# GpSimd makes the shifted copies of VectorE's exponentials with 64-bit integer adds

## The chip, the cores and the metric

The kernel runs on one core of a Trainium2 chip. The metric is the device time of one execution in microseconds (us); the figure quoted is the median of several runs. One execution is also recorded by the hardware profiler, and all profile lines come from that one.

The engines are called PE (TensorE, matrix multiplications; PEld is its loading of weights), ACT (ScalarE), DVE (VectorE), POOL (GpSimd) and SP (SyncE, which only starts DMA transfers here).

## The reference

Two transformer layers that share their weights, on one sequence of 2048 tokens of width 512, with 32 heads of 16 columns and a hidden layer of 1792. All inputs are bf16.

```python
def _A_ref(x, wqkv, wo):                       # attention
    qkv = (x @ wqkv).reshape(B, S, 3, H, Dh).transpose(2, 0, 3, 1, 4)
    q, k, v = qkv[0], qkv[1], qkv[2]
    scores = jnp.einsum("bhqd,bhkd->bhqk", q, k) * (Dh ** -0.5)
    p = _softmax(scores, axis=-1)
    o = jnp.einsum("bhqk,bhkd->bhqd", p, v)
    return o.transpose(0, 2, 1, 3).reshape(B, S, D) @ wo

def _B_ref(x, w1, b1, w2, b2):                 # MLP
    h = _gelu(jnp.einsum("bsd,df->bsf", x, w1) + b1)
    return jnp.einsum("bsf,fd->bsd", h, w2) + b2

x = x + _A_ref(_layernorm(x), A_wqkv, A_wo)
x = x + _B_ref(_layernorm(x), B_w1, B_b1, B_w2, B_b2)
x = x + _A_ref(_layernorm(x), A_wqkv, A_wo)
x = x + _B_ref(_layernorm(x), B_w1, B_b1, B_w2, B_b2)
```

## The kernel before

**Cells and passes.** The attention is cut into cells: one head, 128 keys, 512 queries. 32 heads, 16 key tiles, 4 query chunks and 2 layers give 4096 cells. A pass (`passes`, L1185) is four heads over the key tiles for one query chunk. For a pass, POOL first writes `QP` (`qpad`, L1261, instruction at L1272): the queries, with the columns of the other heads multiplied to zero. PE makes the scores of a cell into one PSUM bank (L1324).

**Two ways to the exponential.** Most cells go to ACT, which takes two or three banks in one instruction (`exps`, L1707, instruction at L1725) and writes `PT` tiles in bf16. The others go to DVE; only five of the sixteen key tiles of a layer (`KD`, L49) may. `next_act` (L1327) and `next_d` (L1335) give the cells out, and `attach` (L1408) puts a DVE cell beside ACT's where a bank is free, so how many cells DVE takes comes out of the planner. DVE's way is bit arithmetic. `dfirst` (L1478, instruction at L1480) scales and shifts the scores and stores them as uint16, so that the bits, read as bf16, are a rough exponential. Three copies of this pattern are needed, with 32, 64 and 96 added to the integer; the four patterns are later weighted (the factors `VW` are multiplied into copies of V, `VC`, written at L1255) and summed by PE, which evens out the error of the rough exponential. So a DVE cell costs four matmuls in the product with V and an ACT cell one (`pvs`, L1743, instructions at L1791).

**The copies.** Two DVE cells make a pair and share a buffer `DU[du][pattern 0..3][cell][512]`: five fixed ones (`DU`, L33) and some that lie in lent parts of K (`kt`) and V (`v`). `dchain` (L1551) makes the copies of a pair: `one` adds 32 to pattern 0, giving pattern 1; `two` adds 64 to patterns 0 and 1 at once, giving 2 and 3. In the kernel before, `one` is a POOL instruction (L1565) if POOL's planned clock is not more than `PSHIFT` behind DVE's, and a DVE instruction otherwise; `two` is always DVE's (L1570). A buffer comes free when the last product of its pair is done.

**Other work.** POOL also normalizes the rows for the layer norms (L747), takes their inverse roots (L726) and divides the attention output (`norm`, L878, POOL's part at L920). DVE evacuates the projections and MLP results from PSUM and does the transposes at the end of a pass (L908, L910, L929). The projections, output projection and MLP (L598) are spread between the attention's matmuls, and PE inserts matmuls of no use (L1312, L1799) to keep its clock up.

**What sets the order.** The order of each engine's instructions is fixed when the program is built. `_Sched` (L245) simulates the five engines with a cost for each operation (`_Op`, L214) and picks the next one by readiness and priority; the semaphore waits are derived from what each operation reads and writes (`_Prog`, L112). `tune` (L391) changes some of the planner's parameters every 24 planned microseconds: entry k of `PICKS` (L100) names the row of `ORDERS` (L86) that holds for stretch k. Each engine then runs its list in order and waits where a semaphore asks for it.

Of the kernel before, what the change touches and what calls it, by code (L numbers as in the profile page):

```python
# [5 lines left out]
ALU = mybir.AluOpType  # L6
# [2 lines left out]
F32 = mybir.dt.float32  # L9
F16 = mybir.dt.float16  # L10
U16 = mybir.dt.uint16

D = 512
H = 32
# [69 lines left out]
PSHIFT = 3  # L84
# [12 lines left out]
    (0.219, 0.8, 99, 1, 0.2, 0.2, 6, 3, 9, 3.5),  # L97
)
STRETCH = 24
PICKS = (2, 0, 0, 6, 8, 2, 5, 1, 0, 5, 1, 0, 7, 5, 1, 0, 0, 7, 2, 5, 9, 1, 8, 7,  # L100
         4, 5, 7, 7, 7, 8, 5, 0, 5, 6, 9, 9, 7, 0, 5, 2, 5, 3, 3, 7, 4, 2, 7, 2,
         0, 9, 7, 7, 3, 3, 0, 2, 10, 10, 4, 4)
LOG2E = 1.4426950408889634
E_SCALE = 0.25 * LOG2E * 128
E_BIAS = 15992.765054484162
SHIFT = 32
VW = (0.83984375, 0.70703125, 0.59375)

ENG_SEM = {"pe": "pe", "act": "act", "dve": "dve", "pool": "pool"}
# [135 lines left out]
class _Sched:  # L245
# [145 lines left out]
    def tune(self):  # L391
        k = min(int(self.clock["act"] // STRETCH), len(PICKS) - 1)
        if k != self.stretch:
            self.stretch = k
            globals().update(zip(KNOBS, ORDERS[PICKS[k]]))
            LATENCY["pe"] = PE
# [79 lines left out]
def bass_interleave_layers__mha_block__dense_activation_gelu__prompt_kernel(  # L476
# [15 lines left out]
    with ExitStack() as es:  # L492
        def sb(shape, dt, name):
            return es.enter_context(nc.sbuf_tensor(name, shape, dt))
# [23 lines left out]
        T["PART1"] = T["K"][0][:, :, :].rearrange("p c s -> p (c s)").bitcast(F32).rearrange("p (g q) -> p g q", g=8)  # L518
        du = sb([128, DU // 2, 4, 2, 512], U16, "du")
        T["DU"] = [du[:, i, :, :, :] for i in range(DU // 2)]  # L520
        if DU % 2:
            half = sb([128, 4, 1, 512], U16, "dh")
            T["DU"].append(half[:, :, :, :])
        late = T["K"][0][:, 2:4, :].rearrange("p c s -> p (c s)").bitcast(U16)
        T["DU"].append(late.rearrange("p (i j q) -> p i j q", i=4, j=2))
        T["DU"].append(T["K"][1][:, :, 1024:2048].rearrange("p i (j q) -> p i j q", j=2).bitcast(U16))
        T["DU"].append(vf[1][:, 8 * H * 17:8 * H * 17 + 4096].bitcast(U16).rearrange("p (i j q) -> p i j q", i=4, j=2))
        T["DU"].append(T["K"][0][:, 0:2, :].rearrange("p c s -> p (c s)").bitcast(U16).rearrange("p (i j q) -> p i j q", i=4, j=2))
        T["DU"].append(vf[0][:, 4096:8192].bitcast(U16).rearrange("p (i j q) -> p i j q", i=4, j=2))
# [58 lines left out]
class _Plan:  # L588
# [658 lines left out]
    def vcopies(self):  # L1247
        T = self.T
        for l in range(NL):
            yield ("cond", lambda l=l: self.pv >= self.lead[l])  # L1250
            for j, kt in enumerate(KD[l]):
                yield ("need", ("V", l, kt, kt // 4))
                src = T["V"][l][:, kt, :, :].rearrange("p h c -> p (h c)")
                for i, w in enumerate(VW):
                    yield _Op("pool", 0.68, lambda e, j=j, i=i, w=w, src=src: e.tensor_scalar(  # L1255
# [295 lines left out]
    def dchain(self, pair):  # L1551


        T = self.T
        cells, du = pair["cells"], pair["du"]
        yield ("cond", lambda: len(cells) == self.cap[du] or pair["full"] or self.starved)
        if self.open is pair:
            self.open = None
        yield ("cond", lambda: pair.get("done", 0) == len(cells))
        n = len(cells)  # L1560
        U = T["DU"][du]
        key = [["DU.%d.%d.%d" % (du, i, j) for j in range(n)] for i in range(4)]
        if self.s.clock["pool"] <= self.s.clock["dve"] + PSHIFT and len(pair["cells"]) == n:
            a, b = U[:, 0, 0:n, :].rearrange("p j q -> p (j q)"), U[:, 1, 0:n, :].rearrange("p j q -> p (j q)")
            one = _Op("pool", 0.15 + 0.45 * n, lambda e, a=a, b=b: e.tensor_scalar(b, a, float(SHIFT), 1.0, op0=ALU.add, op1=ALU.mult),  # L1565
                      reads=key[0], writes=key[1])
        else:
            one = _Op("dve", 0.151 + 0.134 * n, lambda e: e.tensor_scalar(U[:, 1, 0:n, :], U[:, 0, 0:n, :], SHIFT, None, op0=ALU.add),
                      reads=key[0], writes=key[1])
        two = _Op("dve", 0.152 + 0.266 * n, lambda e: e.tensor_scalar(U[:, 2:4, 0:n, :], U[:, 0:2, 0:n, :], 2 * SHIFT, None, op0=ALU.add),  # L1570
                  reads=key[0] + key[1], writes=key[2] + key[3])
        one.port = two.port = True
        yield one
        yield two
        self.duleft[du] = n
        for jj, (pi, kt, a) in enumerate(cells):
            l, seg, g = self.pas[pi][:3]
            gb, ts = self.heads(seg, g)
            j = KD[l].index(kt)
            for i in range(4):  # L1580
                if i == 0:
                    ws, wk = [T["V"][l][:, kt, 8 * gb + 2 * a + t, 0:17] for t in ts], ["V%d.%d" % (l, kt), self.vone(l, kt)]
                else:
                    ws = [T["VC"][:, j, i - 1, 17 * h:17 * h + 17] for h in [8 * gb + 2 * a + t for t in ts]]
                    wk = ["VC.%d.%d" % (j, i - 1)]
                self.dq[(pi, a)].append((ws, U[:, i, jj, :].bitcast(BF16), wk + [key[i][jj]],
                                         ("du", du) if i == 3 else None, i == 3, kt))
# [313 lines left out]
```

## Time and profile before

| what | us |
|---|---|
| median of 3 runs | 1489.72 (1489.6 to 1490.02) |
| span of the profiled execution | 1488.6 |
| PE busy | 1439.3 |
| ACT busy | 1458.5 |
| DVE busy | 1369.4 |
| POOL busy | 857.7 |
| POOL, line L1565, all shapes (552 instructions) | 638.2 |
| DVE, line L1480, all targets (1089 instructions) | 714.8 |

"Busy" is the time in which an engine executes at least one instruction; matmuls overlap, so a busy PE is not PE at its peak. In the rows of the profile that group instructions, the text from left to right is: line of the code, engine, operation, what it writes `<-` what it reads, shapes, how often; then the busy time of the group and the mean time of one instruction in ns; then the idle time of the engine right before these instructions, and what ended it. A group's busy time counts overlapping instructions once, so it can be less than count times mean.

The number of instructions of each kind below comes from the listing of the built program, which has each engine's instructions in their order and no times.

### The profile page before, as it was taken

Reading aid. Unit: us, or ns where it says so; the run is one execution under the profiler, and the core shown is the slowest. Engines: PE = TensorE matmul, PEld = TensorE weight load, DVE = VectorE, ACT = ScalarE, POOL = GpSimd, SP = SyncE. Lnnn points to the kernel's source line nnn. Section 1 sums busy time; section 2 is a strip of 40 time slices with the busy share of each in tenths; the row PEclk is TensorE's granted clock in tenths of the full one; section 3 lists DMA queues with packets and bytes.
Section 4 is the critical chain, followed back from the end, with each engine's and each line's share of the span. In section 5 each row is a group of like instructions: output and inputs, shape, how many; then the busy total and the mean of one; then the engine's idle time right before and its main releaser. Section 6 shows DMA issues by size and latency. Waiting matters only on the chain.

```text
span 1488.6 us, 46137 instructions
## 1 busy us (share of the span) xinstructions
PE 1439.3 (97%) x20011; PEld 433.5 (29%) x20011; DVE 1369.4 (92%) x2340; ACT 1458.5 (98%) x1438; POOL 857.7 (58%) x830
## 2 busy tenths in 40 slices
PE   8999999999999999999999999999999999999998
PEld 3222222222222222222222222222222222344445
DVE  6579999999999999999899999999999999998984
ACT  8999999999999999999999999999999999999995
POOL 5437656567465665556666567656556656654440
PEclk9999999999999999999999999999999999999999
DMA  5100001143120333114421144101143114411433
GB/s 161 40 2 2 2 2 44 37 136 109 29 52 30 117 109 81 39 30 127 118 63 30 46 124 121 34 2 37 40 148 99 37 30 130 143 40 35 148 110 95
DMA packets 145045, 103.38 MB, mean 69 GB/s; under 512 B 37069, under 2 KB 143822, under 8 KB 144846
## 3 DMA queue, kind: packets, MB, share of 16 engines
q1 hardware_dynamic: 144846, 100.44, 23.6%
q8 instruction: 160, 2.62, 0.7%
q14 instruction: 39, 0.32, 0.1%
HBM read 88.61 MB, written 4.19 MB: 62 GB/s over the span
## 4 chain that ended last, share of the span: by engine, by line
ACT 65%; PE 25%; DVE 8%; issue 1%; DMA 0%; SPq 0%; POOL 0%; ACTq 0%
ACT pt L1725 48%; PE ps L598 9%; PE ps L1324 8%; PE ps L1791 8%; ACT q L1725 5%; ACT v L1725 3%; DVE du L1480 3%; ACT g L1076 3%; ACT kt L1725 3%; DVE du L1570 2%; ACT g L1725 2%; ACT L1076 1%; ACT L1725 1%; DMA b1c<-in_B_b_dram 0%; DVE v L906 0%
## 5 line engine op out<-in xcount | busy, mean ns | idle before, releaser
L1725 ACT ACTIVATE pt<-ps 128x1024 bf16<-128x1024 f32 (+1 forms) x1106 | 1123.5, 1146 | 5.1 <-PE ps L1791 2.9
L1565 POOL TENSOR_SCALAR du<-du 128x1024 uint16<-128x1024 uint16 (+1 forms) x404 | 464.4, 1151 | 367.1 <-DVE du L1480 354.4
L1324 PE MATMUL ps<-qp,kt 32*128 32x512 bf16 x4096 | 553.7, 384 | 26.2 <-ACT pt L1725 13.5
L1480 DVE TENSOR_SCALAR du<-ps 128x512 uint16<-128x512 f32 x795 | 520.2, 680 | 31.6 <-PE ps L1324 28.9
L1791 PE MATMUL ps<-pt,v 128*17 128x512 bf16 (+1 forms) x2686 | 358.6, 359 | 5.5 <-ACT pt L1725 2.8
L1791 PE MATMUL ps<-du,vc 128*17 128x512 bf16 (+1 forms) x2646 | 345.0, 360 | 1.1 <-DVE du L1570 0.8
L1324 PEld LDWEIGHTS ps<-qp,kt 32*128 32x128 bf16 x4096 | 144.5, 91 | 596.1 <-ACT pt L1725 189.4
L1570 DVE TENSOR_SCALAR du<-du 128x2048 uint16<-128x2048 uint16 (+1 forms) x404 | 293.9, 739 | 5.0 <-POOL du L1565 4.8
L1799 PE MATMUL ps<-vc,zero 128*17 128x512 bf16 x909 | 179.0, 381 | 0.0
L1791 PE MATMUL ps<-du,v 128*17 128x512 bf16 (+1 forms) x882 | 160.8, 361 | 2.9 <-DVE xt L910 1.6
L1565 POOL TENSOR_SCALAR kt<-kt 128x1024 uint16<-128x1024 uint16 (+1 forms) x94 | 110.6, 1176 | 82.9 <-DVE kt L1480 77.0
L1480 DVE TENSOR_SCALAR kt<-ps 128x512 uint16<-128x512 f32 x186 | 123.3, 681 | 9.3 <-PE ps L1324 8.6
L598 PE MATMUL ps<-xf,wr 128*32 128x512 bf16 (+1 forms) x1888 | 130.6, 365 | 0.3 <-DVE g L1055 0.2
L1272 POOL TENSOR_SCALAR qp<-q,mask 128x512 bf16<-128x512 bf16 (+1 forms) x103 | 84.7, 822 | 63.2 <-PE ps L1324 60.8
L1791 PE MATMUL ps<-kt,vc 128*17 128x512 bf16 (+1 forms) x660 | 119.0, 348 | 1.4 <-DVE kt L1570 1.4
L598 PE MATMUL ps<-wr,g 128*32 128x512 bf16 x1600 | 117.3, 382 | 0.0
L1791 PEld LDWEIGHTS ps<-du,vc 128*17 128x17 bf16 x2646 | 90.9, 89 | 74.3 <-issue 45.5
L1791 PEld LDWEIGHTS ps<-pt,v 128*17 128x17 bf16 x2686 | 87.0, 88 | 87.7 <-issue 57.2
L1725 ACT ACTIVATE q<-ps 128x1024 bf16<-128x1024 f32 (+1 forms) x88 | 96.3, 1144 | 0.0
L1791 PE MATMUL ps<-kt,v 128*17 128x512 bf16 (+1 forms) x381 | 88.7, 363 | 0.9 <-DVE xt L910 0.6
L1565 POOL TENSOR_SCALAR v<-v 128x1024 uint16<-128x1024 uint16 x54 | 63.2, 1170 | 41.0 <-DVE v L1480 37.8
L1055 DVE TENSOR_SCALAR g<-ps,hb1t 128x512 bf16<-128x512 f32 (+1 forms) x112 | 78.8, 705 | 7.2 <-PE ps L598 7.0
(103 smaller groups left out, 1687.9 us busy)
## 6 DMA issues: line engine op xcount, KB each, us to landing
wr<-in_B_w_dram SPq DMA_DIRECT2D x256, 256.0 KB, 2.8
wr<-in_A_wqkv_dram SPq DMA_DIRECT2D x24, 256.0 KB, 2.8
wr<-in_A_wo_dram SPq DMA_DIRECT2D x18, 256.0 KB, 3.0
x<-in_A_x_dram SPq DMA_DIRECT2D x7, 512.0 KB, 4.3
kept<-x SPq DMA_DIRECT2D x4, 512.0 KB, 2.9
x<-kept SPq DMA_DIRECT2D x4, 512.0 KB, 4.0
out_dram<-x SPq DMA_DIRECT2D x16, 128.0 KB, 2.8
g<-in_A_wqkv_dram SPq DMA_DIRECT2D x3, 512.0 KB, 5.2
```

What stands on the lines that cost most here:

```text
L598: return [lambda e, a=a: e.matmul(out[32 * a:32 * a + 32, :], lhsT=lhsT[:, 32 * a:32 * a + 32], rhs=rhs, start=start, stop=stop, tile_posi ...
L1055: yield _Op("dve", 0.21 + n / 966, lambda e, fc=fc, pb=pb: e.tensor_scalar(T["G"][:, fc, q], pb, T["HB1T"][:, fc:fc + 1], None, op0=ALU.ad ...
L1076: lambda e, g=g: e.activation(out=g, in_=g, func=ACT.Gelu_apprx_tanh), reads=gk, writes=gk, prio=2)
L1272: yield _Op("pool", 0.27 + 0.42 * w / 512, lambda e, s=s, q=q, i=i, t=t, w=w: e.tensor_scalar(T["QP"][:, s, w * i:w * i + w], q, T["MASK"] ...
L1324: return (lambda e: e.matmul(o, lhsT=lhsT, rhs=rhs, start=True, stop=True, tile_position=(32 * a, 0)), ["K%d.%d.%d" % (l, gb, kt // 4), "Q ...
L1480: yield _Op("dve", 0.682, lambda e: e.tensor_scalar(u, self.bank(b), E_SCALE, E_BIAS, op0=ALU.mult, op1=ALU.add), reads=["B.%d" % b], writ ...
L1565: one = _Op("pool", 0.15 + 0.45 * n, lambda e, a=a, b=b: e.tensor_scalar(b, a, float(SHIFT), 1.0, op0=ALU.add, op1=ALU.mult), reads=key[0] ...
L1570: two = _Op("dve", 0.152 + 0.266 * n, lambda e: e.tensor_scalar(U[:, 2:4, 0:n, :], U[:, 0:2, 0:n, :], 2 * SHIFT, None, op0=ALU.add), reads ...
L1725: yield _Op("act", 0.065 + 0.4267 * n, lambda e, src=src, dst=dst: e.activation(out=dst, in_=src, func=ACT.Exp, scale=0.25), reads=["B.%d" ...
L1791: op.fns.append(lambda e, o=o, lhsT=q[0][0][m], rhs=q[0][1][:, n * m:n * m + n], a=a, st=st, sp=sp: e.matmul(o, lhsT=lhsT, rhs=rhs, start= ...
L1799: op.fns.append(lambda e, o=self.bank(b)[32 * a:32 * a + 17, :], rhs=rhs, a=a, st=not begun[a], sp=end: e.matmul(o, lhsT=T["ZERO"][:, 0:17 ...
```

## The change

Both `one` and `two` become POOL instructions of another kind, `int64_add`. Four uint16 values that lie side by side are taken as one 64-bit integer, and the constant has 32 (or 64) in each of its four 16-bit fields. DVE makes no copies. The planner gets a cost for the two operations and a new table `PICKS`; with that, the order on all engines is planned again, and how many cells DVE takes comes out anew.

```diff
+I64 = mybir.dt.int64
...
-PICKS = (2, 0, 0, 6, 8, 2, 5, 1, 0, 5, 1, 0, 7, 5, 1, 0, 0, 7, 2, 5, 9, 1, 8, 7,
-         4, 5, 7, 7, 7, 8, 5, 0, 5, 6, 9, 9, 7, 0, 5, 2, 5, 3, 3, 7, 4, 2, 7, 2,
-         0, 9, 7, 7, 3, 3, 0, 2, 10, 10, 4, 4)
+PICKS = (3, 0, 0, 3, 3, 5, 0, 0, 3, 3, 0, 0, 4, 3, 3, 3, 0, 3, 0, 0, 0, 0, 3, 0,
+         3, 0, 0, 0, 0, 0, 0, 0, 0, 0, 0, 1, 3, 3, 0, 3, 4, 5, 4, 0, 7, 3, 0, 3,
+         0, 0, 0, 0, 3, 7, 0, 0, 5, 10, 0, 3)
...
+ONES = 0x0001000100010001
...
-        if self.s.clock["pool"] <= self.s.clock["dve"] + PSHIFT and len(pair["cells"]) == n:
-            a, b = U[:, 0, 0:n, :].rearrange("p j q -> p (j q)"), U[:, 1, 0:n, :].rearrange("p j q -> p (j q)")
-            one = _Op("pool", 0.15 + 0.45 * n, lambda e, a=a, b=b: e.tensor_scalar(b, a, float(SHIFT), 1.0, op0=ALU.add, op1=ALU.mult),
-                      reads=key[0], writes=key[1])
-        else:
-            one = _Op("dve", 0.151 + 0.134 * n, lambda e: e.tensor_scalar(U[:, 1, 0:n, :], U[:, 0, 0:n, :], SHIFT, None, op0=ALU.add),
-                      reads=key[0], writes=key[1])
-        two = _Op("dve", 0.152 + 0.266 * n, lambda e: e.tensor_scalar(U[:, 2:4, 0:n, :], U[:, 0:2, 0:n, :], 2 * SHIFT, None, op0=ALU.add),
+        def words(i, k):
+            u = U[:, i:i + k, 0:n, :]
+            u = u.rearrange("p i j q -> p i (j q)") if k > 1 else u[:, 0, :, :].rearrange("p j q -> p (j q)")
+            return u.bitcast(I64)
+
+        yield _Op("pool", 0.18 + 0.2176 * n, lambda e: e.int64_add(words(1, 1), words(0, 1), SHIFT * ONES),
+                  reads=key[0], writes=key[1])
+        yield _Op("pool", 0.18 + 0.4352 * n, lambda e: e.int64_add(words(2, 2), words(0, 2), 2 * SHIFT * ONES),
                   reads=key[0] + key[1], writes=key[2] + key[3])
-        one.port = two.port = True
-        yield one
-        yield two
```

What the built programs contain:

| instructions | before | after |
|---|---|---|
| cells by DVE (L1480, then L1482) | 1089 | 1166 |
| cells by ACT | 3007 | 2930 |
| ACT exponentials of 3, 2 and 1 cells | 249, 1130, 0 | 197, 1169, 1 |
| `one` and `two` on POOL | 552 and 0 | 600 and 600 |
| `one` and `two` on DVE | 0 and 552 | 0 and 0 |
| pairs of two cells, and of one | 537 and 15 | 566 and 34 |
| other POOL instructions on data | 278 | 278 |
| library loads on POOL | 1 | 321 |
| matmuls | 20011 | 19769 |

The last but one row is not in the code: the building of the program puts an instruction on POOL that names the library of GpSimd routines to be loaded, wherever an instruction needs another library than the one before it. `int64_add` is in library 1, the other arithmetic of this kernel in library 0. Before, there is one such instruction, for library 0, ahead of L608. After, there are 160 for library 1 and 161 for library 0. A stretch of POOL's list after the change (`ISA` without tiles is a library load, `ISA` with tiles an `int64_add`; the listing counts 32-bit elements):

```
L1570 ISA
L1570 ISA du<-du 128x512 x2
L1572 ISA du<-du 128x1024 x2
L1570 ISA du<-du 128x512
L922 ISA
L922 TensorTensor ott<-xt,rc 128x16x16
L1572 ISA
L1572 ISA du<-du 128x1024
L1570 ISA du<-du 128x512
L1572 ISA du<-du 128x1024
L1570 ISA du<-du 128x512
L1572 ISA du<-du 128x1024
L1570 ISA kt<-kt 128x512
L1570 ISA du<-du 128x512
L1572 ISA kt<-kt 128x2x512
L1572 ISA du<-du 128x1024
L1570 ISA du<-du 128x512
L1274 ISA
L1274 TensorScalarPtr qp<-q,mask 128x512
```

## The prediction, made before the changed kernel was run

> **What bounds the kernel now.** I read the page first: the busy shares, then the chain of work that ended last.
>
> ```profile
> PE 1439.3 (97%) x20011; PEld 433.5 (29%) x20011; DVE 1369.4 (92%) x2340; ACT 1458.5 (98%) x1438; POOL 857.7 (58%) x830
> ...
> ACT 65%; PE 25%; DVE 8%; issue 1%; DMA 0%; SPq 0%; POOL 0%; ACTq 0%
> ...
> L1725 ACT ACTIVATE pt<-ps 128x1024 bf16<-128x1024 f32 (+1 forms) x1106 | 1123.5, 1146 | 5.1 <-PE ps L1791 2.9
> ```
>
> ACT executes for 1458.5 of 1488.6 us and waits only 5.1 us ahead of its main group. The exponentials are the bound, PE is close behind, DVE next. POOL has 1488.6 - 857.7 = 631 us of idle time and no share of the chain. The list of waits says what POOL lacks: patterns that DVE has yet to write.
>
> ```profile
> POOL du L1565 <- DVE du L1480: 354.4, 281, 6.7
> ```
>
> So work may be given to POOL until those 631 us are used up. Everything below turns on whether the change asks for more.
>
> **What it takes from DVE and ACT.** The rows of L1570, shapes kept apart, hold 287.6 + 6.3 + 68.4 + 1.2 + 39.6 = 403 us of DVE time; all of it goes. DVE takes 77 more cells (1166 for 1089) at 680 ns, +52 us: DVE falls to about 1369 - 403 + 52 = 1018 us and is far from any bound. ACT has 77 cells fewer. Its work other than exponentials is 43.9 + 3.3 + 5.9 (L1076, L1050), 20.6 (16 table loads of 1283 ns) and 8.1 (copies), 81.8 us; 1458.5 - 81.8 = 1376.7 over 3007 cells is 0.458 us a cell, so ACT loses 35 us. If POOL kept up, the time would be about 1489.7 - 35 = 1455 us. PE's three extra matmuls for each of the 77 cells are 231, against 503 fewer fillers (411 at L1799, 92 at L1312), and cost nothing while PE has those fillers to leave out; without them, 231 in rounds of four at 0.21 us (703.83 less 703.62 is such a spacing in the timeline) would be 12 us.
>
> **What it puts on POOL: the adds.** No `int64_add` is in the trace. The nearest rows are POOL's own additions on the same tiles:
>
> ```profile
> L1565 POOL TENSOR_SCALAR du<-du 128x1024 uint16<-128x1024 uint16 x391 | 454.5, 1164 | 363.6 <-DVE du L1480 351.2 <-DVE mv L721 9.2
> L1272 POOL TENSOR_SCALAR qp<-q,mask 128x512 bf16<-128x512 bf16 x87 | 75.1, 863 | 58.6 <-PE ps L1324 56.5 <-ACT q L825 1.7
> ```
>
> The means are mixed. The timeline of POOL shows the undisturbed length, 1.04 us, and a longer one, as in
>
> ```profile
> 422.45 1.05 POOL L1565 TENSOR_SCALAR v<-v 128x1024 uint16<-128x1024 uint16 x1
> 423.48 0.69 POOL L1272 TENSOR_SCALAR qp<-q,mask 128x512 bf16<-128x512 bf16 x1
> 424.13 1.49 POOL L1565 TENSOR_SCALAR du<-du 128x1024 uint16<-128x1024 uint16 x1
> ```
>
> Taking 0.65 us for 512 elements (the spacing 423.48 to 424.13) and 1.04 for 1024, an element costs 0.76 ns and the start 0.26 us. What is an element of a 64-bit add? If it is the 64-bit word, `one` and `two` of a full pair (256 and 512 words) take 0.455 + 0.65 = 1.1 us; if each 16-bit value, 1.04 + 1.82 = 2.86 us. The listing counts 512 and 1024 elements of 32 bits, and I take that: 0.65 + 1.04 = 1.69 us a pair, 0.455 + 0.65 = 1.1 for a pair of one cell. Sum: 566 x 1.69 + 34 x 1.1 = 994 us, with ends 651 and 1676. POOL's additions of before, 638 us, go. The rest of POOL, 857.7 - 638.2 = 219.5 us, stays, and I count it as 194: the disturbed lengths should go with the DVE copies, and 87 x 0.69 + 16 x 0.48 instead of 84.7 us at L1272, with 58 x 0.77 instead of 53.6 at L747, save 26. So POOL has 194 + 994 = 1188 us of work on data, 80% of the span of before. That alone would fit.
>
> **What it puts on POOL: the library loads.** The listing has 321 of them for one before. POOL's list alternates between adds and `qp`, `ott`, `xln` or `rstd`, in 160 stretches of 7.5 adds and as many of 1.7 others. A load stands between them in order, so nothing on POOL can cover it, and behind it wait the adds, for which PE's products wait, and `qp`, without which no score of the next pass starts. What is one worth? The only one in the trace is ahead of L608:
>
> ```profile
> 0.72 0.20 POOL L607 MEMSET ident<- 128x128 bf16 x1 [0.29 <-POOLq L1886]
> 1.17 0.29 POOL L608 TENSOR_SCALAR_AFFINE_SELECT ident<-ident 128x128 bf16<-128x128 bf16 x1 [0.24 <-POOL ident L607]
> ```
>
> The gap is 0.24 us, but no other library was used before it: this may be a load with nothing to fetch. It is the lower end. For the upper end I look at what a fetch from memory takes in this profile:
>
> ```profile
> x<-in_A_x_dram SPq DMA_DIRECT2D x4, 128.0 KB, 2.1
> ...
> g<-in_A_wqkv_dram SPq DMA_DIRECT2D x3, 512.0 KB, 5.2
> ```
>
> and, another engine exchanging what it computes with,
>
> ```profile
> L1076 ACT ACT_TABLE_LOAD x8 | 10.3, 1283 | 0.1
> ```
>
> The upper end of a single fetch is 0.24 + 5.2 = 5.44 us. The size of a library isn't to be seen. I take the upper end, because a library is code, more than a table, fetched in full and before the next instruction can start; the nearest row is the longest fetch. 320 x 5.44 = 1741 us.
>
> The Trainium skill, page "GPSIMD Engine Reference", section 2.1 "Instruction dispatch", says that the first call to a freshly loaded library pays about 6 us (5.95 measured), with no instruction in the profile to show it. No run here shows it yet; the trace's 0.24 us disagrees if that load fetched anything. By the page the loads are 320 x 5.95 = 1904 us, and the sum below would be 3222 instead of 3059.
>
> **The sum.** POOL becomes the bound: 194 + 994 + 1741 = 2929 us of it. Outside lie what comes before the adds and what follows them: in the trace of before the first L1565 starts at 69.3 us, with POOL busy for about 36 until then (33 idle), and the last ends at 1456.8, 32 before the end, 1 of it POOL's. That is 64 us. POOL still waits at the ends of passes: an `ott` needs a transpose (705 ns), a reciprocal (241) and a last product, some 2 us for each of 64 head groups if no add of the next pair fills them, 0 if they do; I take 1 us, 65 in all. 2929 + 64 + 65 = 3058 us of span; the time before is 1.1 over its span, so **3059 us**. DVE's and PE's waits on POOL cost nothing besides, for they lie inside POOL's time, as long as a pair or two of filled patterns stand ready; five fixed buffers allow it. POOL passes the bound of 1455 us as soon as a load costs (1455 - 1188 - 129) / 320 = 0.43 us, and the time before at 0.54.
>
> **The rivals.**
> 1. *A load costs nothing to speak of* (the lower end; the library change is then not what it says). 320 x 0.24 = 77 us, POOL 1188 + 77 + 129 = 1394: ACT stays the bound and the time is 1455, faster. For it: the one row. Against: that row loads what is presumably there. It decides below 0.43 us a load.
> 2. *A load is like ACT's table load*, 1.28 us: 410 + 1188 + 129 + 1 = 1728.
> 3. *Only one direction fetches*, library 0 staying where it is: 160 x 5.44 + 160 x 0.24 = 909, in all 2227. For it: the 0.24 us row is a load of library 0.
> 4. *A load is two fetches, one behind the other*: 0.24 + 2 x 5.2 = 10.64, 3405 + 1188 + 129 + 1 = 4723.
>
> **How the numbers follow.** Forecast 0.62; rival 1 0.06, rival 2 0.11, rival 3 0.10, rival 4 and other loads over 8 us 0.11. The low end takes in rival 3 and the smallest fetch (0.24 + 2.1 = 2.34 us: 749 + 1188 + 129 = 2066): 2050. The high end takes in the dearest add (3059 + 682 = 3741) and loads of up to 8.6 us: 4200. Half of the 0.11 for dear loads lies within, so 0.78 in all. No change that can be told is under 0.2% of the time, and only a load at 0.5 us gives that: 0.01. Faster is the rest of rival 1, 0.05, slower 0.94.
>
> **What would show it.** Right: POOL heads the chain; ACT, PE and DVE each have half of the span idle, ended by POOL; between an add and the next `qp` or `ott` stands a gap of 5 to 6 us, and the same behind. The gaps in either direction tell rival 3; the start-to-start distance of two adds in a row, 0.65 and 1.04 us, tests the adds. The rows of L1570 on DVE are gone, DVE's busy time is near 1018 us, and L1272 is at 0.69. Wrong: gaps below half a microsecond and ACT at 98%.

## The result and the profile after

The changed kernel takes 3430.94 us (median of 4 runs, 3421.34 to 3436.13), the kernel before on the same chip 1489.87; the ratio is 2.301, 95% interval 2.297 to 2.305. The span of the profiled execution is 3426.7 us.

First the busy times and the chain that ended last, from the page of the changed kernel:

```profile
span 3426.7 us, 46531 instructions
...
PE 1739.7 (51%) x19769; PEld 441.3 (13%) x19769; DVE 1109.7 (32%) x1865; ACT 1478.1 (43%) x1426; POOL 1135.6 (33%) x1478
...
PEclk9766767766676667776667766665567767676778
...
issue 42%; PE 39%; POOL 13%; DVE 4%; ACT 1%; DMA 0%; SPq 0%; POOLq 0%; DVEq 0%
```

No engine is busy for much more than half of the span. POOL, which sets the time, shows 33%, less than ACT, and has 13% of the chain. The word to look at is "issue", 42%: time in which an engine waits for nothing that the profile shows. The same word stands in POOL's groups, whose last columns are the idle time ahead of them and what ended it:

```profile
L1572 POOL INT64_ADD du<-du x438 | 441.1, 1008 | 328.4 <-issue 304.1
L1570 POOL INT64_ADD du<-du x438 | 259.6, 594 | 425.8 <-issue 321.3 <-DVE du L1482 77.7 <-DVE rc L915 6.1
...
L1274 POOL TENSOR_SCALAR qp<-q,mask 128x512 bf16<-128x512 bf16 x87 | 59.4, 683 | 558.6 <-issue 298.5 <-PE ps L1326 128.3 <-PE ps L600 50.7
```

The timeline of POOL (start, length, instruction, idle time before it in brackets) shows what this time is:

```profile
1510.31 0.68 POOL L1274 TENSOR_SCALAR qp<-q,mask 128x512 bf16<-128x512 bf16 x1 [7.12 <-PE ps L600]
1517.20 0.60 POOL L1570 INT64_ADD kt<-kt  x1 [6.21 <-issue]
1517.90 1.04 POOL L1572 INT64_ADD kt<-kt  x1
1518.92 0.61 POOL L1570 INT64_ADD du<-du  x1
1519.62 1.04 POOL L1572 INT64_ADD du<-du  x1
1527.72 0.73 POOL L728 TENSOR_TENSOR rstd<-varr,nhalf 128x2 f32<-128x2 f32 x1 [7.06 <-issue]
1528.44 0.61 POOL L922 TENSOR_TENSOR ott<-xt,rc 128x256 bf16<-128x256 f32 x1
1534.98 0.60 POOL L1570 INT64_ADD du<-du  x1 [5.93 <-issue]
```

Two adds in a row follow at once, and so do `rstd` and `ott`. A gap stands exactly where the listing has a library load, about 7 us on the way to library 0 and 6 us on the way to library 1, and nowhere else in this stretch. The name in the bracket is no guide: the 7.12 us ahead of `qp` are put down to a matmul of PE, and are as long as the gaps with "issue". Over the whole timeline:

| from, to | how many | sum us | mean | shortest | median |
|---|---|---|---|---|---|
| library 0 work, then an add | 160 | 953.7 | 5.96 | 5.58 | 5.92 |
| an add, then library 0 work | 160 | 1159.3 | 7.25 | 6.48 | 7.09 |
| two adds in a row | 950 | 118.1 | 0.12 | | |

Each of the 320 loads in the list has such a gap. It isn't the change from one routine to another as such: where the list has a memset between two adds and no load, nothing stands still.

```profile
380.25 0.60 POOL L1570 INT64_ADD du<-du  x1
380.80 0.66 POOL L630 MEMSET v<- 128x128 bf16 x1
381.08 1.24 POOL L1572 INT64_ADD du<-du  x1
382.25 0.66 POOL L630 MEMSET v<- 128x128 bf16 x1
```

So POOL's time is 1135.6 of data, 2113 of loads and 178 of everything else, together 3427. The other engines wait for it. The list of waits (who waited for whom, us in total, how often, longest):

```profile
ACT pt L1724 <- PE ps L1326: 1485.3, 351, 41.2
DVE du L1482 <- PE ps L1326: 1228.6, 420, 41.1
...
PE ps L1790 <- POOL du L1572: 509.1, 59, 24.1
PE ps L1790 <- POOL du L1570: 496.7, 51, 42.7
...
DVE otn L931 <- POOL ott L922: 246.4, 18, 22.6
```

ACT and DVE wait for scores; PE, which makes them, stands at a product with V whose copies POOL hasn't made, with the next scores behind it in its queue.

### The profile page after: what moved, and what is told of

Same layout as the page of the kernel before. It is cut to its first block, busy times and chain, and to the rows that moved or that the text cites. A ratio compares the mean times of both kernels' runs of the same rounds, so it can differ in the third digit from the quotient of the medians.

```text
span 3426.7 us, 46531 instructions
## 1 busy us (share of the span) xinstructions
PE 1739.7 (51%) x19769; PEld 441.3 (13%) x19769; DVE 1109.7 (32%) x1865; ACT 1478.1 (43%) x1426; POOL 1135.6 (33%) x1478
## 2 busy tenths in 40 slices
DMA packets 145051, 103.42 MB, mean 30 GB/s; under 512 B 37069, under 2 KB 143822, under 8 KB 144846
## 4 chain that ended last, share of the span: by engine, by line
issue 42%; PE 39%; POOL 13%; DVE 4%; ACT 1%; DMA 0%; SPq 0%; POOLq 0%; DVEq 0%
PE ps L1790 15%; PE ps L1326 13%; PE ps L600 10%; POOL du L1572 4%; POOL du L1570 2%; DVE du L1482 2%; POOL qp L1274 2%; POOL kt L1572 1%; POOL xln L749 1%; ACT pt L1724 1%; POOL ott L922 1%; POOL v L1572 1%; PE ps L1314 1%; POOL kt L1570 1%; POOL rstd L728 0%
## 5 line engine op out<-in xcount | busy, mean ns | idle before, releaser
L1482 DVE TENSOR_SCALAR du<-ps 128x512 uint16<-128x512 f32 x849 | 567.6, 686 | 1230.5 <-PE ps L1326 1228.6
L1790 PE MATMUL ps<-du,vc 128*17 128x512 bf16 (+1 forms) x2832 | 451.3, 464 | 617.5 <-POOL du L1572 380.4
L1326 PE MATMUL ps<-qp,kt 32*128 32x512 bf16 x4096 | 633.7, 449 | 222.0 <-DVE du L1482 115.0
L1572 POOL INT64_ADD du<-du x438 | 441.1, 1008 | 328.4 <-issue 304.1
L1570 POOL INT64_ADD du<-du x438 | 259.6, 594 | 425.8 <-issue 321.3
L1790 PE MATMUL ps<-kt,vc 128*17 128x512 bf16 (+1 forms) x708 | 188.3, 440 | 92.4 <-POOL du L1572 59.1
L1482 DVE TENSOR_SCALAR kt<-ps 128x512 uint16<-128x512 f32 x202 | 136.7, 686 | 225.6 <-PE ps L1326 224.9
L1724 ACT ACTIVATE q<-ps 128x1024 bf16<-128x1024 f32 (+1 forms) x77 | 84.0, 1110 | 141.7 <-PE ps L1326 140.0
L1482 DVE TENSOR_SCALAR v<-ps 128x512 uint16<-128x512 f32 x115 | 77.4, 685 | 201.4 <-PE ps L1326 200.9
L1572 POOL INT64_ADD kt<-kt x103 | 104.8, 1018 | 112.8 <-issue 107.2
L1790 PE MATMUL ps<-v,vc 128*17 128x512 bf16 (+1 forms) x402 | 107.5, 435 | 62.8 <-POOL v L1572 25.7
L1798 PE MATMUL ps<-vc,zero 128*17 128x512 bf16 x498 | 129.5, 457 | 0.0
L1724 ACT ACTIVATE kt<-ps 128x1024 bf16<-128x1024 f32 (+1 forms) x75 | 82.6, 1115 | 94.9 <-PE ps L1326 92.9
```

Source lines behind the costliest of these rows:

```text
L1326: return (lambda e: e.matmul(o, lhsT=lhsT, rhs=rhs, start=True, stop=True, tile_position=(32 * a, 0)), ["K%d.%d.%d" % (l, gb, kt // 4), "Q ...
L1482: yield _Op("dve", 0.682, lambda e: e.tensor_scalar(u, self.bank(b), E_SCALE, E_BIAS, op0=ALU.mult, op1=ALU.add), reads=["B.%d" % b], writ ...
L1570: yield _Op("pool", 0.18 + 0.2176 * n, lambda e: e.int64_add(words(1, 1), words(0, 1), SHIFT * ONES), reads=key[0], writes=key[1])
L1572: yield _Op("pool", 0.18 + 0.4352 * n, lambda e: e.int64_add(words(2, 2), words(0, 2), 2 * SHIFT * ONES), reads=key[0] + key[1], writes=ke ...
L1724: yield _Op("act", 0.065 + 0.4267 * n, lambda e, src=src, dst=dst: e.activation(out=dst, in_=src, func=ACT.Exp, scale=0.25), reads=["B.%d" ...
L1790: op.fns.append(lambda e, o=o, lhsT=q[0][0][m], rhs=q[0][1][:, n * m:n * m + n], a=a, st=st, sp=sp: e.matmul(o, lhsT=lhsT, rhs=rhs, start= ...
```

## The experiments

Each is a small edit of one of the two kernels. The theory: the library loads are nearly all of the added 1941 us. The rivals: the order that was planned anew; GpSimd's adds as such; PE's lower clock.

**The new table alone (e1).** The kernel before with the new `PICKS`.

```diff
-PICKS = (2, 0, 0, 6, 8, 2, ...
+PICKS = (3, 0, 0, 3, 3, 5, ...
```

> The kernel before with nothing but the new table PICKS. Loads theory (the 320 library loads, 13.2 us for a pair of them, are nearly all of the 1941 us): the order is no part of it, so 1480 to 1510 us. Rival, the new order is what starves PE and ACT: well over 1600 us.

Measured: 1526.08 us, ratio to the kernel before 1.023 (1.021 to 1.025). The order is not the cause of 1941 us, but the expectation of no effect was wrong: a table made for one set of costs takes 34 us from a kernel with another. ACT waits 17.4 us ahead of its main group instead of 5.1, and DVE gets 1067 cells instead of 1089.

**The same order without loads (e2).** Every `int64_add` becomes an add of library 0 on the same data.

```diff
-            return u.bitcast(I64)
+            return u
...
-lambda e: e.int64_add(words(1, 1), words(0, 1), SHIFT * ONES)
+lambda e: e.tensor_scalar(words(1, 1), words(0, 1), float(SHIFT), 1.0, op0=ALU.add, op1=ALU.mult)
...
-lambda e: e.int64_add(words(2, 2), words(0, 2), 2 * SHIFT * ONES)
+lambda e: e.tensor_scalar(words(2, 2), words(0, 2), 2.0 * SHIFT, 1.0, op0=ALU.add, op1=ALU.mult)
```

> The changed kernel, every engine's order kept, with each int64_add replaced by a uint16 tensor_scalar add on the same data, so that no library changes. GpSimd's work on data grows: 566 x (1.04 + 1.86) + 34 x (0.65 + 1.04) = 1699 us of adds and 173 us of the rest, 1872. Loads theory: GpSimd stays the bound, but at 1872 + 64 for the ends + 65 to 150 for waits = 2000 to 2090 us, though it adds more than the changed kernel does. Rival, GpSimd has too many operations in this order or the fallen TensorE clock holds everything: it stays near or above 3400 us, as the adds have grown by 737 us.

Measured: 2041.04 us (one run). GpSimd's adds became slower and the kernel 1390 us faster. Its busy times and two of its groups (the means mix pairs of two cells with pairs of one):

```profile
PE 1618.5 (79%) x19769; PEld 436.5 (21%) x19769; DVE 1179.7 (58%) x1865; ACT 1470.1 (72%) x1426; POOL 1876.9 (92%) x1478
...
L1572 POOL TENSOR_SCALAR du<-du 128x2048 uint16<-128x2048 uint16 (+1 forms) x438 | 809.4, 1852 | 20.7
...
L1570 POOL TENSOR_SCALAR du<-du 128x1024 uint16<-128x1024 uint16 (+1 forms) x438 | 447.2, 1026 | 39.5 <-DVE du L1482 38.8
```

Now POOL is visibly the bound, at 92%, and the idle time ahead of these two groups, 328.4 and 425.8 us in the changed kernel, is 20.7 and 39.5. The order and the placing on GpSimd are the same in both kernels, so neither explains these 1390 us. PE's lower clock goes along with PE's waiting: over these runs the mean granted clock is 0.71 where PE is busy for 51% of the span, 0.80 at 66% (e3), 0.86 at 79% (here), 0.90 at 83% (e5) and 0.99 at 91% (e7). No run changes the clock alone, but in the changed kernel POOL's data and loads leave only 178 us in which it could matter.

**Fewer loads (e3).** `qp` to DVE, order planned again; 154 loads are left.

```diff
-                yield _Op("pool", 0.27 + 0.42 * w / 512, lambda e, s=s, q=q, ...
+                yield _Op("dve", 0.24 + 0.25 * w / 512, lambda e, s=s, q=q, ...
```

> The changed kernel with the queries' masking (qp, 103 instructions) on VectorE instead of GpSimd; order planned again. 154 library loads are left of 320. Loads theory: 83 pairs of loads fewer at 13.2 us and 67 us of qp fewer, 3427 - 1096 - 67 = 2264, so 2200 to 2400 us. Rival (order or waits between engines): not in proportion to the loads, over 2800 us.

Measured: 2422.07 us (one run), 22 over the range. The time falls by 1009 us for 166 loads. The loads are not dearer: the median gaps are 5.97 and 7.19 us, from 5.92 and 7.09. The gaps with a load in them sum to 479.7 + 568.8 = 1048.5 us instead of 1016, but two of them, 23.6 and 18.9 us long, hold waits as well. The rest of the 158 us above the point estimate is 17 us more of data and some 109 us of other waits: POOL now also waits for DVE, which has `qp` in its queue (the gaps between two adds sum to 231 us, from 118).

**Loads in the kernel before (e5).** Nothing of the change, but 31 trips to library 1 and back, by a tiny add on a scratch tile.

```diff
+                trip = [lambda e: e.int64_add(T["TRIP"][:, 1, :].bitcast(I64), T["TRIP"][:, 0, :].bitcast(I64), 0)] if i == 0 and pi % 3 == 0 else []
-                yield _Op("pool", 0.27 + 0.42 * w / 512, lambda e, s=s, ...
+                yield _Op("pool", 0.27 + 0.42 * w / 512, trip + [lambda e, s=s, ...
```

> The kernel before, copies as they were, with a tiny int64_add on a scratch tile ahead of the queries' masking of every third pass: 31 trips to library 1 and back, 62 loads, 31 x 13.2 = 409 us of GpSimd time for a GpSimd that idles 631 us. Theory (the idle time lies in pieces of 1 to 4 us, a pair of VectorE cells comes about every 2.7 us, and VectorE's queue stands still as soon as it needs a copy): of each 13.2 us some 10 show in the time, 1490 + 31 x 10 = 1800, 1740 to 1900 us. Rival, the idle time takes them up: 1490 to 1530 us.

Measured: 1828.74 us (one run) against 1491.73, 337 us for 31 trips, 10.9 each. On POOL the trips take 187.5 us of gaps on the way out, 6.1 of adds and 228.1 of gaps on the way back, 13.6 us each: its 631 us of idle time hide less than 3 us of a trip. The waits of this kernel show who pays:

```profile
POOL qp L1276 <- issue: 228.1, 31, 7.9
...
DVE du L1574 <- POOL du L1569: 185.2, 28, 13.9
```

31 gaps before `qp`, and DVE's `two`, which waited 4.8 us in all for POOL in the kernel before, waits 185 us, up to 13.9 at a time.

**A planner that knows of the loads (e7).** The changed kernel; POOL's operations get a library, and one that needs the other library is 6.6 us later for the planner.

```diff
+                if e == "pool" and self.lib(th.op) not in (None, self.held):
+                    rdy = max(rdy, self.clock[e]) + LOAD
...
+            if e == "pool" and self.lib(op) is not None:
+                self.held = self.lib(op)
```

> The changed kernel with a planner that knows of the loads: 6.6 us for a change of library, so that GpSimd's work of one library is put together. 58 loads are left, and VectorE takes 972 cells instead of 1166. Loads theory: by the loads alone 3431 - 262 x 6.6 = 1702; by the price of a trip in the kernel before, 10.9 us, on top of 1455 us, 29 x 10.9 + 1455 = 1771; so 1690 to 1800 us. Rival (the adds or the new order have a price of their own that the loads don't explain): over 1900 us.

Measured: 1784.99 us (one run). With 58 loads the time is in the range that the loads gave. Gathering the work by library helps by 1646 us, but the kernel stays 295 us slower than the one before: `qp` and `ott` are due in every pass, and in this order 29 round trips are left. How much of the 295 us lies in them and how much in the fewer cells of DVE (972) was not tried apart.

**One load (e4).** All arithmetic of library 0 moves to DVE: `qp`, `xln`, `ott`, `vc`, and in place of the power -1/2 a bit trick with two Newton steps.

```diff
-        eng, cost = ("dve", 0.4) if quick else ("pool", 0.77)
+        eng, cost = ("dve", 0.4) if quick else ("dve", 0.49)
...
-            yield _Op(*(("pool", 0.63 * w / 512) if pool else ("dve", 0.153 + 0.262 * w / 512)), ...
+            yield _Op(*("dve", 0.153 + 0.262 * w / 512), ...
...
-        yield _Op("pool", 0.37 + 0.18 * n, lambda e: e.tensor_tensor( ... op=ALU.pow), ...
+        yield _Op("dve", 0.2, lambda e: e.tensor_scalar(w.bitcast(I32), v.bitcast(I32), 1, None, op0=ALU.logical_shift_right), ...
+        yield _Op("dve", 0.2, lambda e: e.tensor_scalar(y.bitcast(I32), w.bitcast(I32), -1.0, 1597463007.0, op0=ALU.mult, op1=ALU.add), ...
+        for _ in range(2):
+            yield _Op("dve", 0.2, lambda e: e.tensor_tensor(out=w, in0=y, in1=y, op=ALU.mult), ...
+            yield _Op("dve", 0.2, lambda e: e.scalar_tensor_tensor(out=w, in0=w, scalar=-0.5, in1=v, op0=ALU.mult, op1=ALU.mult), ...
+            yield _Op("dve", 0.2, lambda e: e.scalar_tensor_tensor(out=y, in0=w, scalar=1.5, in1=y, op0=ALU.add, op1=ALU.mult), ...
```

> The changed kernel with all arithmetic of library 0 on VectorE (qp, xln, ott, vc, and the inverse root as a bit trick with two Newton steps in place of pow); GpSimd keeps the int64_adds and memsets, and one library change is left. Loads theory: GpSimd has about 960 us of work, VectorE about 1050 + 31 + 24 + 20 + 12 + 35 = 1170, ACT is the bound again with 35 us less than before: 1445 to 1480 us, faster than the kernel before. Rival, GpSimd's adds are too slow or come too late by themselves: over 1500 us.

Measured: 1538.4 us, ratio 1.031 (1.030 to 1.033): the loads are gone and with them 1893 us, but it is slower than the kernel before, outside what was expected. The time lies where the rival (the adds are too slow by themselves) had put it, but e8 and e10 below have the same adds and are faster, so it isn't the adds. ACT is busy for 93% of the span, and ACT's main group waits 42.6 us where it waited 5.1. The planner's costs were too low, as these groups of e4 show (mean ns, against 407, 332 and 407 that the planner counts, which takes 83 ns off a DVE cost for overlap):

```profile
L1285 DVE TENSOR_SCALAR qp<-q,mask 128x512 bf16<-128x512 bf16 x87 | 46.6, 536 | 6.5 <-PE ps L1337 6.1
...
L933 DVE TENSOR_TENSOR ott<-xt,rc 128x256 bf16<-128x256 f32 x56 | 35.2, 628 | 1.1
...
L760 DVE TENSOR_SCALAR xln<-x,rstd,nmr 128x512 bf16<-128x512 bf16 x60 | 29.8, 514 | 0.9 <-DMA kt<-xln 0.4
```

**The same, planned for what it does (e8).** e4 with these costs, three priorities and a `PICKS` of its own.

```diff
-EVAC = 0.4
+EVAC = 9
...
-RUSH = 1
+RUSH = 2
...
-                yield _Op("dve", 0.24 + 0.25 * w / 512, lambda e, s=s, q=q, ...
+                yield _Op("dve", 0.42 + 0.2 * w / 512, lambda e, s=s, q=q, ...
...
-        s.spawn(self.qpad(), 4)
+        s.spawn(self.qpad(), 1)
```

> The kernel e4 (all arithmetic of library 0 on VectorE, one library change) with its order planned for what it does: VectorE's costs from e4's profile (qp 0.54, xln 0.51, ott 0.63, the small steps 0.28 to 0.38 us, where the planner had 0.12 to 0.41), VectorE no longer made to wait for GpSimd in the plan, three priorities changed (EVAC 9, RUSH 2, the masking 1) and a table PICKS of its own. Theory (e4's 46 us over the kernel before are its order, not GpSimd's adds or VectorE's load): ACT busy 97% or more, 1460 to 1488 us, faster than the kernel before. Rival, VectorE has too much to do in time for ACT whatever the order: 1500 us or more.

Measured: 1491.57 us, ratio 1.000 (0.999 to 1.001). The new plan (costs, priorities and table together) was worth 47 us, all of e4's loss. The expected gain stayed out: ACT is busy for 96% of the span, and the time lies between the expected range and the rival's.

**The opening back on GpSimd (e10).** What comes before the first add anyway may use library 0 without another load.

```diff
+QPOOL = 6
...
-        eng, cost = ("dve", 0.4) if quick else ("dve", 0.6)
+        eng, cost = ("dve", 0.4) if quick else ("dve", 0.66) if ph else ("pool", 0.77)
...
-                yield _Op("dve", 0.42 + 0.2 * w / 512, ...
+                yield _Op(*(("pool", 0.27 + 0.42 * w / 512) if pi < QPOOL else ("dve", 0.5 + 0.2 * w / 512)), ...
```

> As e8, but what GpSimd can do of library 0 before its first add stays on GpSimd: the layer norms of the first layer's input, the weighted copies of V of layer 1, the queries' masking of the first six passes. One change of library is left, between these and the adds. Order planned again with VectorE's costs from e8 and a price of a load, priorities LATE 0.5, QUEUE 6 and RUSH 3. In e8's first 75 us ACT is busy for 54 us, in the kernel before for 68; e8 is level with the kernel before. Theory (with the loads gone, what is left between e8 and the expected 1455 us is its opening and its order): 14 us or more below e8, 1460 to 1480 us, faster than the kernel before. Rival, VectorE's added work in the middle holds ACT back: no better than 1488 us.

Measured: 1477.6 us, ratio 0.991 (0.990 to 0.993): 0.9% faster than the kernel before and far faster than the changed one; the gain is small but clear of the noise. The reason given was largely not the right one: in the first 75 us ACT is busy for 57.4 us, against 54.2 in e8, so 3 us of the 14 come from there. DVE takes 1198 cells instead of 1156 and the order is another one; how the rest divides between these was not tried.

Part of why the opening stays poor (ACT is busy for 67.8 us of it in the kernel before) shows in the first instruction of library 0, which makes `ident`. These are the lines of e4, e8 and e10:

```profile
8.41 0.28 POOL L611 TENSOR_SCALAR_AFFINE_SELECT ident<-ident 128x128 bf16<-128x128 bf16 x1 [7.47 <-issue]
8.40 0.28 POOL L609 TENSOR_SCALAR_AFFINE_SELECT ident<-ident 128x128 bf16<-128x128 bf16 x1 [7.46 <-issue]
8.32 0.28 POOL L619 TENSOR_SCALAR_AFFINE_SELECT ident<-ident 128x128 bf16<-128x128 bf16 x1 [7.38 <-issue]
```

In the kernel before, the same instruction starts at 1.17 us after a gap of 0.24. PE's first matmul, which waits for a memset behind it, starts at 9.13 us in e10 and at 1.99 in the kernel before. So these three kernels pay a second load, and nothing covers it. They are the three whose list on POOL ends with an `int64_add`; the other seven end with work of library 0, and there the gap is 0.24 to 0.50 us. This fits a library that stays in place from one execution to the next; it was not tried separately.

The adds of e10 are those of the changed kernel, without the gaps:

```profile
PE 1420.5 (96%) x19802; PEld 433.8 (29%) x19802; DVE 1228.6 (83%) x2242; ACT 1424.8 (97%) x1445; POOL 1024.7 (69%) x1289
...
L1596 POOL INT64_ADD du<-du x449 | 456.3, 1018 | 33.8
L1594 POOL INT64_ADD du<-du x449 | 271.1, 605 | 258.9 <-DVE du L1506 208.6 <-DVE mv L732 18.6 <-DVE rstd L753 9.3
```

All kernels with their loads in one view ("in the body" leaves out the one ahead of `ident`, which every kernel has); counted from the changed kernel, each load taken away is worth 5.9 to 6.3 us in e3, e7, e4 and e10 (whose work on DVE differs, too):

| kernel | loads in the body | time us |
|---|---|---|
| changed | 320 | 3430.94 |
| e3 | 154 | 2422.07 |
| e7 | 58 | 1784.99 |
| e2 | 0 | 2041.04 |
| e4 | 1 | 1538.4 |
| e8 | 1 | 1491.57 |
| e10 | 1 | 1477.6 |
| before with trips (e5) | 62 | 1828.74 |
| before, new table (e1) | 0 | 1526.08 |
| before | 0 | 1489.87 |

## Why the prediction was right, and where it was off

The mechanism was right: the adds fit into POOL's time and the loads don't. The forecast was 3059 us, the measured time 3431. The difference is about that of one term, the loads; two smaller misses cancel.

- *The loads*, 320 x 5.44 = 1741 us, were 2113: 5.96 us in one direction and 7.25 in the other, 6.6 on average. This is the term that was mis-sized, by 372 us. The upper end that was built from the longest fetch was not an upper end. That it came so near is in part luck: the price was that of a 512 KB transfer, but the 320 loads show no transfer at all. The changed kernel has 145,051 DMA packets and 103.42 MB, and e2, the same list without a change of library, 145,046 and 103.38. What a load spends its 6 to 7 us on stays open. The Trainium skill, "GPSIMD Engine Reference", section 2.1 "Instruction dispatch", says 5.95 us for the first call to a freshly loaded kernel (a routine of GpSimd) and that nothing in the profile shows it; the 5.96 us ahead of the adds and the word "issue" agree. The way back to library 0, 7.25 us, is longer than that figure; the estimate by the page was 3222 us.
- *The adds* were 994 us by counting 32-bit elements; the six rows give 962. The start-to-start distances were to be 0.65 and 1.04 us and are 0.70 and 1.02. The unit isn't confirmed by this: the three lengths that occur (0.40, 0.61, 1.04 us) fit a start of 0.19 us, below the 0.26 taken, and 1.7 ns a 64-bit word, above the 1.52 of two elements at 0.76, and the two errors nearly cancel. The other work was counted as 194 and takes 173.5. POOL's data in all: 1188 forecast, 1135.6 measured, 52 less.
- *Ends and waits*, 64 + 65, are 178, 49 more. 372 - 52 + 49 = 369 is the whole distance from 3058 to 3427. Two slips in the working change nothing: 64 head groups at 1 us are 64, not 65, and by the prediction's own sum 4200 us stand for loads of 9.0 us, not 8.6.
- *Rival 1*, a load for nothing, read the gap of 0.24 us at L608 as a load. The library was most likely there already: in e4, e8 and e10 the same load takes 7.4 to 7.5 us. No load that changed the library was under 5.58 us.
- *Rival 3*, only one direction, is excluded by the 160 gaps ahead of library 0's work, the longer ones. *Rivals 2 and 4* by the shortest and the median gap.
- *The signs named in advance*: gaps in both directions and the shorter `qp` (649 ns over both shapes, from 822; the forecast was 0.69 for the larger, measured 0.683) came as described. So did the idle halves: ACT, PE and DVE idle for 57, 49 and 68% of the span, PE waiting for POOL and the other two for PE. "POOL heads the chain" did not come: a load has no record, so the chain books it as "issue" and as PE. DVE's 1018 us were 1110, mostly because its instructions overlap less: the busy times of its groups add up to 1499 us before, 129 more than the engine's, and to 1166 after, 56 more. The sum took 403 us of the groups away as if none of it had overlapped.
- *1455 us if POOL kept up* was not tested as it stands: no run has the `int64_add`s and library 0's work on POOL without the loads. The nearest kernels, with library 0's work on DVE, gave 1538, 1492 after planning anew, and 1478 with the opening back on POOL. The sum left out that an order fits one set of costs.

## What to carry to other kernels

Look through the built program for instructions that the source doesn't have; here 320 of them, on one engine and in order, cost more than the whole kernel. Don't alternate operations of different libraries on GpSimd, at some 13 us a round trip here: give it the operations of one library for long stretches and put the rest on another engine, or leave the new instruction alone. Look at both ends of the list, too: a kernel that began with one library and ended with the other paid a load at its start. Idle time of an engine is worth only as much as the buffers around it: 58 busy per cent did not mean that a stall of 13 us would be hidden.

## What the runs showed of the hardware that was not expected

- The load is paid at every change, in both directions, 160 times each, with little scatter (5.58 to 6.76 us towards library 1; 6.48 to 8.21 towards library 0, median 7.09, and one gap of 15.96 that holds a wait). Nothing is kept of the library that was left: in e5 library 0 is away for a single add of 0.2 us, and its way back still takes 6.71 to 7.85 us.
- Naming the library that is in place costs next to nothing: 0.24 to 0.50 us ahead of `ident` in seven kernels, against 7.38 to 7.47 in the three that end with the other library.
- `int64_add` takes 0.40 us for 128 words of 64 bits, 0.61 for 256 and 1.04 for 512, some 1.7 ns a word. The uint16 adds of e2 on the same bytes take 1.05 and 1.90 us (256 and 512 words' worth), so packing saves 42 and 45%.
- Beside DVE's copies POOL is slower: `qp` (128x512) took 863 ns before, 876 in e1 and 818 in e5, all with these copies on DVE, and 683 after, 700 in e2 and 685 in e7, without them, with no instruction of its own changed.
